# A spectral mixing and SwiGLU kernel: its build-time scheduler, its kinds, and the engine of its setup copies are changed

## The chip, the cores and the metric

The kernel runs on one core of a Trainium2 chip. The metric is the device time of one execution in microseconds. The core's engines run side by side: TensorE (PE) multiplies matrices and accumulates into eight PSUM banks, VectorE (DVE), ScalarE (ACT) and GpSimd (POOL) work on elements, SyncE (SP) and some others issue DMAs. Each engine works through its own list of instructions in the order in which the program was built; an instruction waits on semaphores for others.

## The reference

```python
def _attn_ref(x):                      # x: 8 x 3008 x 256, float32
    X = np.fft.fft(x, axis=1)
    X = np.fft.fft(X, axis=2)
    return X.real

def _moe_ref(x, w_gate, w_val, w_out): # 24064 tokens, 256 -> 1536 -> 256
    g = x @ w_gate
    silu = g * (1.0 / (1.0 + np.exp(-g)))
    val = x @ w_val
    return silu * val @ w_out
```

The real part of a two-dimensional Fourier transform of each of eight sequences is fed, token by token, through a gated feed-forward layer.

## The kernel before, in words

**Symmetry.** A row of the transform at one frequency and the row at the mirrored frequency share an even part and an odd part. The kernel keeps these two parts, transposed, in tiles Pt (even) and Qt (odd) of up to 512 columns. The transform over the 256 features is folded into the weights: Wp is the cosine transform of the weights, Wq the sine transform, Wm is -2 Wq with some rows masked, Wg is Wm of the gate halved. A column's plus side is Wp Pt + Wq Qt, its mirror, the minus side, is the same with the odd part's sign turned. There are 24 tiles of columns.

**Units.** The feed-forward layer is walked tile by tile, and in a tile by twelve blocks f of 128 hidden rows. Such a unit (t, f) has a gate bank and a value bank in PSUM. How a bank's two sides are made is its kind, a digit in the table KINDS (one line for each tile: twelve gates, twelve values, twelve products):

- kind 0: matmuls with Wp and Wq give the plus side, which is read; a third matmul with Wm on top turns the bank into the minus side.
- kind 1: after the Wp matmul DVE copies the even part out and adds a constant row to it (L1123); after the Wq matmul the bank is the plus side, and DVE makes the minus side as 2 x even - bank (gate L1177, value L1191). Two matmuls.
- kind 2: ACT writes the constant row into the bank first (the seed, L1113), the matmul with Wp adds to it, ACT copies the even part out (L1120); then one matmul with Wg or Wm, and DVE's difference. Two matmuls.

ACT takes the silu of both sides (L1138, L1169, L1180). The plus product is D, made by DVE from the bank (L1161), or P, where ACT copies the value out (L1154) and POOL multiplies (L1157). The minus products of two blocks are multiplied together on POOL (L1198), or on DVE where the value has kind 0. The products h are then multiplied with the output weights Wo, 12 matmuls of 256 columns for each 128 tokens (class OWork, L1225); ACT evicts the result (L1231, L1234) and SP stores it.

**The next sequences.** While the units run, POOL folds the rows of the sequences to come (L207 to L231), TensorE transforms them (transform_op, L1356), ACT copies the odd half out of PSUM (L1367) and DVE writes the results into Pt and Qt (the puts, L1381; those of the first sequence are L683).

**The prologue.** Up to the first units all is ordered by hand, in the lines L287 to L738. The trigonometric tables are computed on the chip: angles (L395), magnitude (L399), then cosine and sine on ACT, a negated copy of table columns on ACT (L411), a weighting with a per-row constant (weigh, L408). place() copies rows of the input into PSUM with 0/1 matmuls (L469), sums() adds them on DVE (L478), giving SA for the rows at the front and SC for the rest; heads() makes the first columns from them (L487, L488). fold_d (L535) and direct (SBc, L572) fold over features; half_folded and unfolded are the first sequence's transform matmuls; half_w (L503 to L507) makes the first 512 columns of Wp and Wq, load_w (L421) issues the DMAs of the weights on POOL's queue, columns in three groups. The second and third groups (weight_op, L1410 to L1416) are made while the first units run, as are the second half of the tables (angle_op, weigh_op, odd_op, L1436 to L1487).

**The scheduler.** From the first unit on, every instruction is an entry of class Sched: its engine, an assumed length, what it reads and writes, a category. The entry's due time is the sum of TensorE lengths before it plus a shift of its category (SHIFT). The planner plays the assumed lengths through: for every engine it looks among the entries due within WINDOW of that engine's first one and takes the one that can start earliest. It thereby fixes the order of each engine's list and which PSUM bank or work buffer each entry gets. Delays for semaphores (SEM), for the end of an instruction behind its issue (TAIL) and for a second waited-for engine (EVENT), and when each engine comes free (BEGIN, EARLY), are constants:

```python
o.at = o.clock + SHIFT[o.cat][min(5, int(o.clock / 96))]
t = x.end + SEM[e] if x.eng != e else x.free if e == "PE" else x.end
```

Of the kernel before, what the change touches and what calls it, by code (L numbers as in the profile page):

```python
# [12 lines left out]
F32 = mybir.dt.float32  # L13
# [17 lines left out]
EARLY = {**{("Q", i): 14.0 for i in range(2)}, **{("S", i): 14.0 for i in range(6, 11)}}  # L31
KINDS = [
    "000000000000 000000000000 DDDDDDDDDDDD",
    "000000000000 001111001111 DDDDDDDDDDDD",
    "000000000000 111111111111 DDDDDDDDDDDD",
    "000200022200 121211211211 DPDDDDDDPDDD",
    "000002000220 121122111221 DDDDDDDDDDDD",
    "000000002020 212112112111 DDPDDPDDDDDD",
    "000002020200 121122221111 DDDDDPDDDDPD",
    "220000002200 121212111111 DDDDDDDDPDDD",  # L40
    "200000000000 121112111122 DDDDPDPDDDDD",
    "200220020200 112111121212 DDPDPDDDDPDD",
    "020200000022 111111212211 DPPDPDDDPDDP",
    "000002002000 121111121111 DDPPDDDPDDPD",
    "022200002002 112121112112 DDDDDDPPDPDD",
    "000220200200 121111221211 PDDDDDDPPDDD",
    "000000200002 112211212111 DDPDDPDDDDDD",
    "200222002000 111122211111 DDPDDDDDDPDD",
    "200020000200 111122111211 DDDDDPPDPDDD",
    "220000200002 111121121121 PDDDDDPDDPDD",  # L50
    "022200200020 111112221111 DPPDDDPDDDDP",
    "002002000200 212111111211 DDDPPPDDDDDP",
    "020222000002 111111111111 PDPDPDDDDPPD",
    "222022000020 111111111122 DPDPDDDDDPDD",
    "202000000200 111121111112 PDDPPPDDDDDP",
    "202020202022 112211111212 DDDDPDPDDPDD",
# [8 lines left out]
def kernel(  # L65
# [248 lines left out]
    fall_c(0, 1, q)  # L314

# [181 lines left out]
    def half_w(h, k, pool, nm):  # L497
# [6 lines left out]
        if k:  # L504
            nc.scalar.copy(dst[:, :, fs], ps)
        else:
            nc.vector.tensor_copy(dst[:, :, fs], ps)  # L507
# [56 lines left out]

    def direct(k):
# [19 lines left out]
    load_w(0, (1,))  # L585
    d_tables()
# [3 lines left out]
    if 0:  # L590
        warm(0)
# [7 lines left out]
    X3c = XC.rearrange("p a q d -> p (a q d)")  # L599
# [1010 lines left out]
```

## Time and profile before

| | us |
|---|---|
| median of 3 runs | 611.87 (611.11 to 611.89) |
| the profiled execution | 612.4 |
| its span, first to last instruction | 610.5 |
| PE busy | 602.7 (99%) |
| ACT busy | 567.3 (93%) |
| DVE busy | 558.0 (91%) |
| POOL busy | 541.8 (89%) |
| DMA moved | 57.72 MB, mean 95 GB/s |

The busy times are shares of the span. A matmul's end is modelled in the profile and overlaps the next one's start, so a TensorE that is shown busy is not TensorE at its peak; starts of successive matmuls say more. A group row of the profile reads: line, engine, operation, tiles written and read, shape, count, then busy time and the mean length in ns, then the idle time of the engine just before and what ended it. A row of the timeline reads: start, length (both us), engine, line, operation, and in brackets an idle stretch before it. The chain of waits follows the work that ended last back to the start. A row of windows gives the stretch, its length, and busy time with counts of PE, weight loads, DVE, ACT and POOL, the granted TensorE clock, the share of the DMA engines and GB/s. In this kernel's profile one instruction's length on ACT or DVE includes a part that overlaps the next one's, so here too starts are the better measure of what an engine can take.

### The profile page before, as it was taken

The page shows a single profiled execution, that of the slowest core. Times are in us where ns is not written, and L with a number is a line of the kernel's source. Part 1 is how long each engine was busy: PE and PEld are TensorE (multiplying, and loading weights), DVE is VectorE, ACT ScalarE, POOL GpSimd, SP SyncE. Part 2 cuts the span into 40 slices and gives each one's busy share as a digit, 9 for nine tenths or more (in the row PEclk, how much of TensorE's full clock was granted, in tenths as well). Part 3 has the DMA queues.
Part 4 walks back from the last instruction along what each step waited for, and adds up shares of the span by engine and source line. Part 5 has one row for each costly group of instructions (what it writes and reads, how often), then busy time and mean ns, then how long its engine had stood idle before and what let it go on. Part 6 is the DMA issues. An engine that isn't in the chain of part 4 may idle for free.

```text
span 610.5 us, 12689 instructions
## 1 busy us (share of the span) xinstructions
PE 602.7 (99%) x4071; PEld 395.1 (65%) x4071; DVE 558.0 (91%) x1028; ACT 567.3 (93%) x1104; POOL 541.8 (89%) x498
## 2 busy tenths in 40 slices
PE   8999999999999999999999999999999999999997
PEld 6546666666666666666666666666666666666686
DVE  8999998988999998998999898999999899999882
ACT  7687659999999999999999999999999999999995
POOL 8888999999889999999999999998999868766772
PEclk9999999999999999999999999999999999999999
DMA  9955536344514423445214411235211111211112
GB/s 226 143 101 109 151 104 183 99 125 130 146 53 107 132 60 117 116 129 130 62 46 116 123 49 60 72 84 152 59 48 53 45 53 47 61 44 55 58 54 79
DMA packets 50737, 57.72 MB, mean 95 GB/s; under 512 B 7256, under 2 KB 37724, under 8 KB 50670
## 3 DMA queue, kind: packets, MB, share of 16 engines
q1 hardware_dynamic: 47016, 53.78, 32.2%
q0 software_dynamic: 3216, 2.36, 2.9%
q10 hardware_dynamic: 438, 0.77, 0.5%
q8 instruction: 32, 0.52, 0.4%
q14 instruction: 35, 0.29, 0.2%
HBM read 29.43 MB, written 24.65 MB: 89 GB/s over the span
## 4 chain that ended last, share of the span: by engine, by line
PE 90%; ACT 2%; DVE 2%; POOL 2%; DMA 2%; issue 1%; ACTq 0%; POOLq 0%
PE ps L1057 46%; PE ps L1225 40%; PE ps L1356 4%; DMA XA<-in_moe_w_val_dram 2%; PE ps L641 1%; POOL EOA L535 1%; ACT ps L1113 0%; ACT sv0q L1169 0%; DVE hm L1185 0%; DVE rr L395 0%; DVE hp L1161 0%; POOL XA L421 0%; ACT sv1q L1169 0%; POOL W L421 0%; ACT wk3s L1180 0%
## 5 line engine op out<-in xcount | busy, mean ns | idle before, releaser
L1057 PE MATMUL ps<-Pt,Wp 128*128 128x512 bf16 (+2 forms) x576 | 206.9, 374 | 0.7 <-DVE Qt L683 0.3
L1225 PE MATMUL ps<-Wo,hm 128*128 128x256 bf16 (+2 forms) x1140 | 165.1, 272 | 0.0
L1225 PE MATMUL ps<-Wo,hp 128*128 128x256 bf16 (+2 forms) x1140 | 164.5, 272 | 0.4 <-ACT wk4s L1231 0.2
L1057 PE MATMUL ps<-Qt,Wq 128*128 128x512 bf16 (+2 forms) x427 | 156.4, 375 | 0.0
L1225 PEld LDWEIGHTS <-hm 128*128 128x128 bf16 (+2 forms) x1140 | 111.8, 98 | 59.4 <-issue 3.0
L1225 PEld LDWEIGHTS <-hp 128*128 128x128 bf16 (+2 forms) x1140 | 111.8, 98 | 56.3 <-issue 4.3
L1198 POOL TENSOR_TENSOR hm<-sv0q 128x1024 bf16<-128x1024 f32 (+2 forms) x68 | 126.7, 1863 | 22.0 <-ACT sv0q L1169 11.2
L1198 POOL TENSOR_TENSOR hm<-sv1q 128x1024 bf16<-128x1024 f32 (+2 forms) x68 | 126.7, 1864 | 20.3 <-ACT sv1q L1169 12.7
L1113 ACT ACTIVATE ps<-bc,w 128x512 f32<-128x512 bf16 (+2 forms) x149 | 110.4, 755 | 0.7
L1057 PE MATMUL ps<-Qt,Wm 128*128 128x512 bf16 (+2 forms) x293 | 104.4, 375 | 0.2 <-DVE hp L1161 0.2
L1057 PEld LDWEIGHTS <-Wp 128*128 128x128 bf16 x576 | 56.2, 98 | 32.5 <-issue 1.7
L1169 ACT ACTIVATE sv0q<-ps 128x512 f32<-128x512 f32 (+2 forms) x102 | 70.6, 713 | 1.2 <-PE ps L1057 0.8
L1169 ACT ACTIVATE sv1q<-ps 128x512 f32<-128x512 f32 (+2 forms) x90 | 64.1, 718 | 2.9 <-POOL hm L1198 2.0
L1057 PEld LDWEIGHTS <-Wq 128*128 128x128 bf16 x427 | 41.6, 98 | 26.8 <-issue 3.7
L1057 PEld LDWEIGHTS <-Wm 128*128 128x128 bf16 x293 | 28.5, 98 | 11.7 <-issue 0.2
L207 POOL TENSOR_TENSOR SDf<-XA 128x1020 f32<-128x1020 f32 x14 | 33.0, 2360 | 0.7 <-DMA XC<-in_x_dram 0.7
L1057 PE MATMUL ps<-Qt,Wg 128*128 128x512 bf16 (+2 forms) x80 | 29.7, 371 | 0.0
L217 POOL TENSOR_TENSOR Af<-EOf 128x516 f32<-128x516 f32 (+1 forms) x22 | 24.5, 1112 | 0.3
L214 POOL TENSOR_TENSOR EOf<-SDf 128x512 f32<-128x512 f32 (+1 forms) x22 | 24.1, 1097 | 0.0
L211 POOL TENSOR_TENSOR EOf<-SDf 128x512 f32<-128x512 f32 (+1 forms) x22 | 24.0, 1091 | 0.0
L207 POOL TENSOR_TENSOR SDf<-XC 128x1020 f32<-128x1020 f32 (+1 forms) x8 | 18.8, 2356 | 2.3 <-DMA XA<-in_x_dram 2.3
L1356 PE MATMUL ps<-Tab,St 128*128 128x376 bf16 (+1 forms) x64 | 20.0, 322 | 0.0
(434 smaller groups left out, 1410.5 us busy)
## 6 DMA issues: line engine op xcount, KB each, us to landing
XA<-in_x_dram SPq DMA_DIRECT2D x30, 256.0 KB
XA<-in_x_dram SPq DMA_DIRECT2D x112, 64.0 KB
XC<-in_x_dram SPq DMA_DIRECT2D x30, 120.0 KB
XC<-in_x_dram SPq DMA_DIRECT2D x105, 32.0 KB
bc<-br SPq DMA_DIRECT2D x21, 128.0 KB
out_dram<-wk8s SPq DMA_DIRECT2D x15, 128.0 KB
St<-Fc SPq DMA_DIRECT2D x14, 128.5 KB
out_dram<-wk2s SPq DMA_DIRECT2D x11, 128.0 KB
```

What stands on the lines that cost most here:

```text
L207: tt(F[:, :, 1:D], up[:, :, 1:D], down[:, :, D - 1:0:-1], op=Alu.add)
L211: tt(E[:, :, 0:P], F[:, :, P:0:-1], F[:, :, P:D], op=Alu.add)
L214: tt(O[:, :, 0:P], F[:, :, P:0:-1], F[:, :, P:D], op=Alu.subtract)
L217: tt(Af[r], EOf[r, :, 0:2, :], EOf[r, :, 2:4, :], op=Alu.add)
L535: ptt(EOA[:, eo, a0:a0 + 2, :, 0:P], s_[:, :, :, P:0:-1], s_[:, :, :, P:D], op=(Alu.add, Alu.subtract)[eo])
L641: nc.tensor.matmul(ps[:, e], Z0[:, q, k, :], Tab[:, c, q, 0, e], start=False, stop=True, skip_group_check=True)
L1057: nc.tensor.matmul(ps[:, :n], Wt[:, gv, fs], src[:, :n], start=start, stop=stop, skip_group_check=True)
L1113: nc.scalar.activation(bank(k)[:, :self.wp], bc[self.t][:, :self.wp], AF.Copy, scale=w0[:, gv, self.f:self.f + 1])
L1169: return lambda: nc.scalar.activation(self.silu(self.sm, w), src()[:, :w], AF.Silu)
L1198: lambda: nc.gpsimd.tensor_tensor(tiles_of(t)[1][:, f - 1:f + 1, :w], pair(self.vm)[:, :, :w, 1], pair(self.vm)[:, :, :w, 0], op=Alu.mult),
L1225: nc.tensor.matmul(bank(ko)[:n, j * D:(j + 1) * D], hts[t][minus][:, f, c:c + n], Wo[:, f, :], start=(f == 0), stop=(f == nF - 1))
L1356: nc.tensor.matmul(ps[:, cols], l, r_, start=(i == 0), stop=(i == len(mms) - 1), skip_group_check=True)
```

## The change

1. **Kinds.** The table is another one: gates of kind 0, 1, 2 were 208, 0, 80 and become 195, 37, 56; values 16, 203, 69 become 18, 190, 80; products made by ACT and POOL 61 become 72.
2. **The planner.** Shifts come in 24 bins of 24 us in place of 6 of 96 (the old ones were the same in all bins). An engine other than PE that uses its own earlier result is charged its end and a semaphore, and this counts as a wait. Lengths are changed, some ends get their own delay (lat), WINDOW, TAIL, EVENT, BEGIN, EARLY and the ring's start are other constants. Where the value is of kind 0 and the gate is not, the plus product is entered in the unit's second half.
3. **Setup work from DVE to ACT**: the casts of Wp (half_w and weight_op), magnitude in angle_op (as an absolute value), weigh_op, odd_table. Halving Wm of the values moves from unit 37 to 25, making Wg from 24 to 13.
4. **The prologue's order.** half_folded(0, 2) goes ahead of place(); start_acc(1), the first fold_d(1) and half_folded(1, 0) go earlier; the clearing of unused rows is split in two, one DMA right behind the loads and one behind a memset that comes earlier; load_w(0, (1,)), which loads the value columns of the first weight group, and d_tables come later; first_columns computes what the heads need with two small additions, so that they need not wait for all of SC; half_w(0, 0) goes ahead of unfolded(1), half_w(0, 1) behind row0; the last sum of SC goes behind transform(0, 0, (1,)).

The core of the diff:

```diff
@@ quarter_rows
-        tt(B_[:, 1], O[:, 0:2, 0:P], O[:, 2:4, 0:P], op=Alu.subtract)
+        tt(B_[:, 1, :, 1:P], O[:, 0:2, 1:P], O[:, 2:4, 1:P], op=Alu.subtract)
@@ half_w
-        if k:
-            nc.scalar.copy(dst[:, :, fs], ps)
-        else:
-            nc.vector.tensor_copy(dst[:, :, fs], ps)
+        nc.scalar.copy(dst[:, :, fs], ps)
@@ prologue
+    clear_rest(0, xf[:, 7 * D:8 * D])
...
+    hc = tp.tile([P, 2, 2, 1], F32, name="hc")
+    def first_columns():
+        for a in range(2):
+            vtt(hc[:, a], psC[a][:, :, 0:1], XC0[:, 2 + a, ::-1, 0:1], op=Alu.add)
...
-    load_w(0, (1,))
-    d_tables()
     sums(SA, 1, XA, psA)
     start_acc(0)
     half_folded(0, 0)
+    half_folded(0, 2)
     psC = place(XC0, putC, 2, ((psG, "g"), (psV, "v")))
-    half_folded(0, 2)
-    for a in (0, 2):
-        fold_d(1, a)
+    start_acc(1)
+    fold_d(1, 0)
+    half_folded(1, 0)
+    zeros = Af.rearrange("p a b d -> p (a b d)")[:, 0:D]
+    nc.gpsimd.memset(zeros, 0.0)
+    clear_rest(1, zeros)
+    load_w(0, (1,))
+    d_tables()
+    fold_d(1, 2)
     direct(0)
     direct(1)
-    start_acc(1)
+    first_columns()
...
-    for a in (0, 2):
-        half_folded(1, a)
+    half_folded(1, 2)
     load_w(1)
...
-    heads(nc.gpsimd, SC[:, 0, 0, :, 0:1], SC[:, 0, 1, :, 0:1], CEc)
+    heads(nc.gpsimd, hc[:, 0], hc[:, 1], CEc)
...
-    for k in range(2):
-        half_w(0, k, psO, "o")
+    half_w(0, 0, psO, "o")
     unfolded(1, SBc)
     for q in range(2):
         row0(0, q, acc[1][q])
-    sums(SC, 1, XC0, psC)
+    sums(SC, 1, XC0, psC, (0,))
     transform(0, 0, (1,), acc)
+    half_w(0, 1, psO, "o")
+    sums(SC, 1, XC0, psC, (1,))
@@ planner
-    WINDOW = {"DMA": 14.0, "PE": 9.378, "ACT": 14.0, "DVE": 12.28, "POOL": 11.566, "SP": 5.558}
+    WINDOW = {"DMA": 5.66, "PE": 7.62, "ACT": 14.0, "DVE": 14.0, "POOL": 14.0, "SP": 7.13}
-    TAIL = {"PE": 0.163, "ACT": 0.118, "DVE": 0.08, "POOL": 0.02, "SP": 0.0, "DMA": 0.0}
+    TAIL = {"PE": 0.163, "ACT": 0.099, "DVE": 0.083, "POOL": 0.044, "SP": 0.0, "DMA": 0.0}
-    EVENT = 0.06
-    BEGIN = {"DVE": 1.2, "ACT": 0.7, "POOL": 14.0, "PE": 0.0, "SP": -4.0}
+    EVENT = {"ACT": 0.055, "DVE": 0.072, "POOL": 0.06, "PE": 0.03}
+    BEGIN = {"DVE": 0.6, "ACT": 1.3, "POOL": 13.1, "PE": 0.0, "SP": -6.6}
-                o.at = o.clock + SHIFT[o.cat][min(5, int(o.clock / 96))]
+                o.at = o.clock + SHIFT[o.cat][min(23, int(o.clock / 24))]
-                    t = x.end + SEM[e] if x.eng != e else x.free if e == "PE" else x.end
+                    t = x.free if x.eng == e and e == "PE" else x.end + SEM[e]
-                        if g != e and g != "x":
+                        if (g != e or e != "PE") and g != "x":
-        return n / 1200 + (0.094 if sbuf else 0.063) + 0.12 * ptr
+        return n / 1200 + (0.088 if sbuf else 0.0605) + 0.1245 * ptr
-                S.add("ACT", act_us(self.wp, 1) - 0.01, fn, r=[self.bc, (("w0",), 0)], w=[k], new=[k[0]], cat=cat,
+                S.add("ACT", act_us(self.wp, 1), fn, r=[self.bc, (("w0",), 0)], w=[k], new=[k[0]], cat=cat, lat=0.08,
-                S.add("ACT", act_us(self.wp) - 0.025, by_act, r=[k], w=[e], new=[e[0]], cat="esc" if gv else "egc")
+                S.add("ACT", act_us(self.wp), by_act, r=[k], w=[e], new=[e[0]], cat="esc" if gv else "egc")
-    FOLD_US = (2.0, 1.06, 1.06, 1.15, 1.24, 1.55)
+    FOLD_US = (2.475, 1.047, 1.047, 1.057, 1.204, 1.345)
@@ setup during the units
-                nc.vector.tensor_copy(dst[:, gv, fs], bank(ko))
+                nc.scalar.copy(dst[:, gv, fs], bank(ko))
-        S.add("DVE", 0.6, lambda: magnitude(raO[:, ch], rrO[:, ch]), ...
+        S.add("ACT", 0.72, lambda: nc.scalar.activation(raO[:, ch], rrO[:, ch], AF.Abs), ...
-        S.add("DVE", 0.45, lambda: weigh(NOO, NTAB), w=[(("Tab",), ("o", 1))])
+        S.add("ACT", 0.52, lambda: nc.scalar.activation(Tab[:, 1, 1, :, NOO:NTAB], Tab[:, 1, 1, :, NOO:NTAB], AF.Copy, scale=wC), ...
-        nc.vector.tensor_copy(Tab[r, c, :, :, NCE:NCE + GH], src[:, :, ::-1] if half else src)
+        nc.scalar.copy(Tab[r, c, :, :, NCE:NCE + GH], src[:, :, ::-1] if half else src)
-        if i == FIRST + 1:
+        if i == 2 * nF + 1:
             S.add("ACT", 1.36, lambda: nc.scalar.activation(Wm[:, 1], Wm[:, 1], AF.Copy, scale=-0.5), ...
-        if i == 2 * nF:
+        if i == nF + 1:
             S.add("DVE", 0.5, lambda: vts(Wg[:, 0], Wm[:, 0], scalar1=-0.5, scalar2=None, op0=Alu.mult), ...
```

More of the change, by code (lines that the diff above doesn't have):

```diff
@@ L57 @@
+    "000212122211 111122111111 PPPDPPDPPDDD",
 ]
@@ L902, in run @@
             lanes = [-9.0] * 8
[L903 removed]
+            ring = -2.0
             def slot_time(s, e):
@@ L966, in ready @@
                         own = max(now, key=lambda g: RANK.get(g, 0))
-                        at = max([at] + [waits[g][1] + EVENT for g in now if g != own])
+                        at = max([at] + [waits[g][1] + EVENT[e] for g in now if g != own])
                 if commit:
@@ L1431, in weight_op @@
             else:
-                S.add("DVE", 0.6, even, r=[ko], w=[(("Wp",), (fc, gv))])
+                S.add("ACT", act_us(T), even, r=[ko], w=[(("Wp",), (fc, gv))])
     raO = SDf.rearrange("p a d -> p (a d)")[:, 0:4 * G].rearrange("p (c q n) -> p c q n", c=2, q=2)
@@ L1474, in d0_op @@
         r = [(("st", b), k) for k in range(2)] if part else [(("cp", b), (q, 0)) for q in range(2)]
-        S.add("POOL", 0.2, fn, r=r, w=[(("Z0",), part)])
+        S.add("POOL", 0.147, fn, r=r, w=[(("Z0",), part)])
     def halve_tables():
```

136 lines of the change are left out of this document (65 added, 71 removed), and 28 rows, old and new, of the table SHIFT.

## The prediction

> **What bounds the kernel now.** I read the busy totals first, then the windows by stage, then the chain of waits, then the timeline around the stalls it shows.
>
> ```profile
> PE 602.7 (99%) x4071; PEld 395.1 (65%) x4071; DVE 558.0 (91%) x1028; ACT 567.3 (93%) x1104; POOL 541.8 (89%) x498
> 0.00:25.00 25.00, 22.47 (x157) 15.49 (x158) 21.99 (x74) 15.78 (x27) 19.82 (x42) 1.00 0.87 182
> 25.00:50.00 25.00, 23.94 (x142) 11.74 (x140) 24.14 (x43) 21.68 (x41) 22.13 (x35) 1.00 0.65 116
> 50.00:92.00 42.00, 41.76 (x280) 27.41 (x278) 40.61 (x64) 26.99 (x50) 38.85 (x41) 1.00 0.49 128
> 92.00:250.00 158.00, 157.67 (x1060) 103.03 (x1058) 145.59 (x267) 151.71 (x293) 153.08 (x137) 1.00 0.42 116
> 250.00:600.00 350.00, 349.85 (x2380) 231.40 (x2378) 324.41 (x582) 348.13 (x690) 306.66 (x247) 1.00 0.26 73
> PE 90%; ACT 2%; DVE 2%; POOL 2%; DMA 2%; issue 1%; ACTq 0%; POOLq 0%
> ```
>
> In a window row the columns behind the length are PE, weight loads, DVE, ACT and POOL with their counts, then the clock granted to TensorE (1.00 throughout). TensorE fills 99% of the span and 90% of the chain: it is the bound. But from 250 to 600 us ScalarE is busy 348.13 of 350 (0.505 us for each of its 690 instructions), so the kernel stands on two limits at once there, with DVE at 93%. Before 92 us it is the other way round: DVE is nearly full (24.14 of 25, 40.61 of 42) and ScalarE has 9.2 + 3.3 + 15.0 = 27.5 us idle.
>
> TensorE's busy time overstates its work, since the modelled ends overlap. Its work is better read from starts:
>
> ```profile
> 44.96 3.36 PE ps L1057 x16
> 137.27 1.31 PE ps L1225 x12
> 300.41 0.38 PE L1057 MATMUL ps<-Qt,Wq 128*128 128x512 bf16 x1
> 300.63 0.38 PE L1057 MATMUL ps<-Pt,Wp 128*128 128x512 bf16 x1
> 53.79 0.59 PE L1057 MATMUL ps<-Qt,Wm 128*128 128x512 bf16 x2
> 54.62 0.27 PE L1225 MATMUL ps<-Wo,hp 128*128 128x256 bf16 x1 [0.24 <-ACT wk4s L1231]
> 581.53 0.30 PE L1057 MATMUL ps<-Qt,Wg 128*128 128x328 bf16 x1
> 581.73 0.30 PE L1057 MATMUL ps<-Qt,Wq 128*128 128x328 bf16 x1
> ```
>
> A 512-column matmul costs 0.216 us (300.41 to 300.63), an output one 1.31 / 12 = 0.109, a 328-column one 0.138 by its width. A distance longer than the pitch is a stall: two matmuls from 53.79 should have ended at 54.22, the next began at 54.62, so 0.40 was lost; the last stall of this kind, at 581.53, lost 0.20 - 0.14 = 0.06. Between these two lie all but one of the 53 stalls over 60 ns that stand behind 50 us; together they are 6.35 us. Ahead of 50 us it is 4.4 us. These two sums, and the matmul columns themselves, are all that the change can work on, unless it brings new stalls.
>
> **The change, part by part.**
>
> *Kinds.* Counting the tables: gates of kind 0/1/2 go from 208/0/80 to 195/37/56, values from 16/203/69 to 18/190/80, P products from 61 to 72. Kind 0 takes three matmuls, 1 and 2 take two: -13 for the gates, +2 for the values, so 11 fewer, which by tile widths is ten of 512 columns, two of 320, and one more of 480. At 0.216 each this is **-2.2 us** on the engine that bounds. No cover is needed for it, unless TensorE then waits.
>
> The other engines, in tiles 3 to 23:
>
> ```profile
> L1113 ACT ACTIVATE ps<-bc,w 128x512 f32<-128x512 bf16 x130 | 98.0, 768 | 0.7
> 303.89 0.74 DVE L1123 SCALAR_TENSOR_TENSOR wk9s<-bc,w,ps 128x512 f32<-128x512 bf16 x1
> 304.55 0.68 DVE L1177 SCALAR_TENSOR_TENSOR wk10s<-wk4s,ps 128x512 f32<-128x512 f32 x1
> 305.46 1.27 POOL L1157 TENSOR_TENSOR hp<-wk0s,wk3s 128x512 bf16<-128x512 f32 x1
> ```
>
> Kind 2 falls there from 149 to 127 (each a seed and an even copy on ScalarE) and 11 value copies come: -44 + 11 = -33 ScalarE instructions, at 0.505 us -16.7 us. DVE gains 31 even copies of kind 1 (304.55 - 303.89 = 0.66 us each), 9 gate differences and loses 11 products (about 0.6 each by starts): +19.3 us. POOL gains 11 products of 1.27: +14 us. So ScalarE's near-full state ends, and DVE, 324.41 of 350 in the late window, comes to about 338 there with its share of the 19.3 (350 of the 515 us behind 92, so 13), and to 344 with all of it. POOL goes from 306.66 to about 317. None passes TensorE's 350, so I charge them nothing by themselves; what cover they lose is in the stalls below.
>
> *The planner.* Lengths of copies and seeds drop their discounts (a 512-column copy 0.465 to 0.487, a seed 0.600 to 0.612), same-engine results cost a semaphore step, priorities get 24 bins, windows change. Nothing in this adds a matmul; it changes who waits in the 6.35 us of stalls. ScalarE's relief removes the cause of those stalls that end on a seed, an eviction or a plus-side silu; those that end on DVE (products, differences) do not go, and get worse by DVE's +19.3. Bounds: all of it goes (-6.3), or it doubles (+6). I take a third gone, **-2.0**: nearer to the first, as the fullest engine is relieved by more than half of what TensorE has to spare, and the others are not filled.
>
> *Prologue.* Rows around the first units:
>
> ```profile
> 13.80 0.67 PE L469 MATMUL ps<-XC,putC 128*128 128x512 f32 x1 [1.16 <-DVE SA L478]
> 12.50 0.73 POOL L421 DMA_DIRECT2D W<-in_moe_w_val_dram  x1
> W<-in_moe_w_val_dram POOLq DMA_DIRECT2D x1, 256.0 KB, 4.6
> XA<-in_moe_w_val_dram POOLq DMA_DIRECT2D x2, 256.0 KB, 9.6
> 20.17 0.68 DVE L507 CAST Wp<-ps 128x512 bf16<-128x512 f32 x1
> 20.77 1.28 DVE L478 TENSOR_TENSOR SC<-ps,XC 128x512 f32<-128x512 f32 x2
> 22.09 1.27 DVE L683 TENSOR_TENSOR Qt<-ps,od 128x188 bf16<-128x188 f32 x6
> 23.41 0.77 PE L1057 MATMUL ps<-Pt,Wp 128*128 128x480 bf16 x3 [0.35 <-DVE Qt L683]
> 20.34 0.20 POOL L487 TENSOR_TENSOR CEc<-SC 128x2 bf16<-128x2 f32 x1 [2.21 <-DVE SC L478]
> 22.54 9.81 DMA XA<-in_moe_w_val_dram
> 32.40 0.62 PE ps L1410 x2
> ```
>
> Steady units begin at 23.41, behind the Qt puts that begin at 22.09 on DVE. After the change the Wp cast (20.77 - 20.17 = 0.60) is on ScalarE, and one of the four SC sums (1.28 / 2, about 0.6) stands behind the puts: DVE's list ahead of them is 1.2 us shorter, two tiny first-column additions put back about 0.2, and TensorE's own order (unfolded(1) now behind half_w(0,0), half_w(0,1) behind row0) takes some more. By the list the puts start near 21.4. The matmuls put in front of place C (half_folded(0,2), 13.80) fill the 1.16 us that TensorE waits there. I take **-0.5**. Against it: POOL issues W's value columns about 1.4 us later (12.50 to some 13.9), behind two fold_d, a memset and the first clear; SP's stores of zeros for XC go ahead of that and share the queues. With the 4.6 us of its own row it lands near 18.5 and half_w(0,0) needs it at 19; with the 9.6 us of the later value columns it lands at 23.5, and TensorE's order is stuck at half_w with unfolded(1) behind it: +3.9. Other end -1.3, the whole of DVE's 1.2 and the rest of the wait. I stand near the own row.
>
> *Second and third weight columns.* POOL waits 2.21 us at 20.34 for the SC sums before it issues them; the heads now read the first-column sums, so both issues come about 1.9 us earlier. In the chain the value columns' 9.81 us from 22.54 end in the weight matmuls at 32.40. TensorE's stalls ahead of these two groups (at 29.0 and 31.7, 0.57 and 0.53) can both go: **-1.0**; bounds 0, if the transfers wait in the same crowd (DMA share 0.87 and 0.65 in the first windows), and -1.1.
>
> *Masks, weights and tables to ScalarE.* The nearest rows:
>
> ```profile
> L1413 DVE CAST Wp<-ps x4: 678/685/692, 25.4 to 33.0; 128x512 bf16<-128x512 f32 x4
> L1416 ACT CAST Wq<-ps x4: 586/596/606, 25.9 to 33.5; 128x512 bf16<-128x512 f32 x4
> L411 ACT ACTIVATE Tab<-Tab x2: 823/829/835, 9.5 to 13.1; 128x752 bf16<-128x752 bf16 x2
> L1484 DVE COPY Tab<-Tab x4: 356/943/1511, 44.5 to 51.8; 64x752 bf16<-64x752 bf16 x4
> L408 DVE TENSOR_SCALAR Tab<-Tab,wC x1: 1292/1292/1292, 37.6 to 37.6; 128x752 bf16<-128x752 bf16 x1
> L399 DVE TENSOR_SCALAR SDf<-XA x2: 535/582/629, 26.0 to 31.6; 128x752 int32<-128x752 int32 x2
> ```
>
> Two Wp casts, four more (L1413), two magnitudes, one weigh, four table copies leave DVE: 6 x 0.685 + 2 x 0.58 + 1.29 + 4 x 0.94 = 10.3 us. On ScalarE they cost 6 x 0.596 + 7 x 0.83 = 9.4 us. Tile 2's new kinds add nine seeds and nine copies there, 18 x 0.505 = 9.1. Together 18.5 of the 27.5 us that ScalarE idles before 92 us, so it fits, though less so where it is needed: the silus of the first tiles stand behind these casts. TensorE hardly stalls there on DVE even now, so the relief is worth little. **0**, bounds +3 (three table operations of 0.83 and a cast caught in front of silus) and -0.8 (the stalls at 38.9 and 54.0).
>
> The Trainium skill, "ScalarE: Activation LUTs", Rules for kernel authors, tells the author to put such work on VectorE, per element up to about 3x faster in bf16. The rows above do not bear that out for these shapes (0.596 on ScalarE against 0.685 on DVE for the cast); by the rule the step would not be free, and that result is the last rival.
>
> *Wm's halving* moves from unit 37 to 25, Wg from 24 to 13: one instruction each, beside other work, nothing. *Tail:* the last output products are the same, 0.
>
> **Sum.** -2.2 - 2.0 - 0.5 - 1.0 = -5.7 us. The profiled execution took 612.4 us (span 610.5, 1.9 around it), 0.5 above the median of 611.87. So 606.7 as profiled, 606.2 as a median.
>
> **Rivals.**
> (A) The planner buys nothing: the stalls after 50 us stay as they are, only matmul columns and the prologue count: -3.7, 608.2. For it: each stall is small (0.06 to 0.4 us) and scattered, so no one engine owns them. Against it: ScalarE at 348.13 of 350.
> (B) DVE takes ScalarE's place. A kind 1 gate holds its PSUM bank through an even copy, a matmul, a difference and a silu of both sides, two of these on DVE; with DVE near 98% late, banks come free late and the next unit's first matmul waits. From four microseconds of stall growth on it eats the gains (-3.7 without the stall term); with stalls doubled, +6, 614, and up to 616 with POOL's +14 beside it. Against it: by sums no engine is full.
> (C) W's value columns land late and the prologue loses instead of gaining: landing 8.5 us after the issue, +2.8 in place of -0.5, the rest as forecast, 609.5. For it: the value columns behind took 9.6. Against it: the same chunk took 4.6.
> (D) Moved work costs three times DVE's time on ScalarE: 10.3 x 3 = 31 us, with tile 2's 9.1 it is 40 in 27.5 idle: 12.5 over, 606.7 + 12.5 = 619.
>
> **How the numbers follow.** 0.2% (1.2 us) is about what a measurement of this kernel tells from no change: 610.65 to 613.1. Chances: forecast 0.55, A 0.20, C 0.09, B 0.14, D 0.02. Faster: the forecast, nearly all of A (0.18) and half of C make 0.78. Same: 0.07 from the rest of A and C and the weak end of B. Slower: 0.15. The low end takes two thirds of the stalls (-4.2), the prologue -1.3, the weight waits -1.1, the early relief -0.8 and the columns -2.2: -9.6, 602.3. The high end goes past A and most of C, to 610.7; B and D above it hold 0.16.
>
> **What would show it.** Right: 11 fewer L1057 matmuls, ScalarE's late window under 340 of 350, steady units at about 22.8, no stall at the weight matmuls near 30 us, stalls after 50 us near 4 us. Wrong: DVE over 97% late and TensorE waiting on L1123, L1177 or L1161 (B); TensorE waiting on W ahead of 20 us (C); ScalarE full before 92 us with silus late (D); the stall sum above 6 us.

## The result

The changed kernel takes 607.81 us (median of 6 runs, 607.02 to 609.88) against 611.73 (6 runs, 610.78 to 612.93): ratio 0.9941, 95% interval 0.9921 to 0.9961, 0.6% faster and clear of the 0.2% that can be told. Forecast were 606.2 in a range of 602.3 to 610.7. The profiled execution took 607.03 us, span 605.1, against 612.4 and 610.5. All that follows compares these two. They are 5.4 us apart, the medians 3.9: the profiled execution of before is slower than its median, the changed kernel's faster, so the rows below show somewhat more of a gain than there is.

The busy totals, the five windows and the chain of the changed kernel, columns as before:

```profile
PE 594.9 (98%) x4060; PEld 393.2 (65%) x4060; DVE 563.6 (93%) x1043; ACT 566.6 (94%) x1102; POOL 550.0 (91%) x508
0.00:25.00 25.00, 20.96 (x154) 13.87 (x155) 20.57 (x73) 15.95 (x27) 21.93 (x45) 1.00 0.98 197
25.00:50.00 25.00, 22.23 (x130) 10.60 (x129) 18.11 (x30) 23.60 (x46) 19.68 (x32) 1.00 0.59 111
50.00:92.00 42.00, 42.00 (x275) 26.92 (x273) 38.12 (x63) 38.45 (x72) 36.38 (x39) 1.00 0.41 113
92.00:250.00 158.00, 158.00 (x1077) 104.86 (x1076) 151.12 (x277) 149.33 (x292) 154.35 (x139) 1.00 0.44 117
250.00:600.00 350.00, 350.00 (x2420) 235.72 (x2418) 335.72 (x604) 338.36 (x668) 317.70 (x258) 1.00 0.27 75
PE 93%; DMA 4%; POOL 1%; ACT 1%; SPq 1%; issue 0%; DVE 0%; DVEq 0%
```

The gain is behind 92 us: 1077 matmuls where there were 1060, 2420 where there were 2380, in the same stretches, with TensorE shown busy throughout. Ahead of 50 us the changed kernel is worse: 154 + 130 matmuls against 157 + 142, and DMA has become 4% of the chain. In distances between starts, beyond the pitch and counted from 60 ns up as in the prediction (profiled executions):

| | before | changed | difference |
|---|---|---|---|
| matmul columns | | | -2.2 |
| stalls ahead of 50 us | 4.0 | 8.3 | +4.2 |
| stalls behind 50 us | 6.4 | 0.8 | -5.5 |
| distances under 60 ns, all | 6.9 | 5.4 | -1.6 |
| last matmul ends | 607.0 | 601.7 | -5.3 |

(The small distances are what is left of TensorE's whole distance to its pitches, 17.4 and 14.5 us, without the stalls. The rows add up to -5.1; 0.2 is not placed.)

Most of the -1.6 is not the change's. Out of TensorE's first 52 matmuls, a stretch of the timeline before and then changed:

```profile
4.20 1.38 PE L341 MATMUL ps<-sel 128*128 128x128 bf16 x11
4.30 1.17 PE L348 MATMUL ps<-sel 128*128 128x128 bf16 x18
```

These matmuls of 128 columns start 0.107 us apart at first and 0.056 us apart later. The step comes at 7.0 us before and at 4.2 us in the changed kernel; in the seven other profiled kernels with this order of the prologue and this issue of W it comes between 4.5 and 6.8 us, so it differs from one execution to the next. From TensorE's first matmul (1.02 us in both) to the first unit the changed kernel takes 1.1 us more, although its stalls there are 2.5 us more: some 1.4 us of the small distances lie ahead of the first unit, and only some 0.4 us behind it (the 0.2 that is not placed among them).

Where the time ahead of 50 us goes is read from the changed kernel's timeline (rows of several engines, in order of time), its DMA issues (the last figure is us to landing) and its chain:

```profile
9.43 0.76 SPq L318 DMA_DIRECT2D XC<-XC  x1
13.26 0.82 PE L527 MATMUL ps<-Tab,EOb 128*128 128x377 bf16 x4 [1.07 <-ACT EOb L540]
13.79 0.73 POOL L428 DMA_DIRECT2D W<-in_moe_w_val_dram  x1
14.60 3.77 SPq L190 DMA_DIRECT2D XC<-in_x_dram  x7
18.24 0.22 POOL L494 TENSOR_TENSOR CEc<-hc 128x2 bf16<-128x2 f32 x1
19.73 0.38 PE L510 MATMUL ps<-W,CD 128*128 128x256 bf16 x2 [1.14 <-DMA W<-in_moe_w_val_dram]
22.35 1.27 DVE L690 TENSOR_TENSOR Qt<-ps,od 128x188 bf16<-128x188 f32 x6 [1.33 <-ACT od L685]
23.79 1.18 PE L1085 MATMUL ps<-Pt,Wp 128*128 128x480 bf16 x5
27.07 0.83 ACT L1470 ACTIVATE SDf<-XA 128x752 f32<-128x752 f32 x1 [0.35 <-DVE XA L402]
28.41 0.36 PE L1085 MATMUL ps<-Pt,Wp 128*128 128x480 bf16 x1 [0.49 <-ACT wk2s L1198]
34.96 0.61 PE L1441 MATMUL ps<-XA,CD 128*128 128x512 bf16 x2 [1.64 <-DMA XA<-in_moe_w_val_dram]
```

```profile
XA<-in_moe_w_val_dram POOLq DMA_DIRECT2D x2, 256.0 KB, 12.9
W<-in_moe_w_gate_dram POOLq DMA_DIRECT2D x1, 256.0 KB, 6.3
W<-in_moe_w_val_dram POOLq DMA_DIRECT2D x1, 256.0 KB, 5.9
```

```profile
20.44 14.47 DMA XA<-in_moe_w_val_dram
```

Of before, the clears and the row loads in the timeline, and W's gate columns:

```profile
15.82 1.51 SPq L605 DMA_DIRECT2D XC<-Af  x2
17.38 4.51 SPq L190 DMA_DIRECT2D XC<-in_x_dram  x2
W<-in_moe_w_gate_dram POOLq DMA_DIRECT2D x1, 256.0 KB, 4.6
```

The matmuls put ahead of place C now wait themselves, 1.07 us at 13.26 for a copy on ScalarE, where TensorE waited 1.16 us before. W's value columns land 5.9 us behind their issue, not 4.6, and hold TensorE 1.14 us (1.7 to 2.4 us in those seven other kernels); DVE has its shorter list done and now waits 1.33 us for ScalarE's copy of TensorE's later result. Steady units begin at 23.79 (before: 23.41, with a first matmul at 22.70). The heads no longer wait and the third weight group is issued at 20.44, 2.1 us earlier; but it takes 14.47 us in place of 9.81 and lands 2.6 us later than before. By the trace's landings twelve of this DMA's sixteen parts are there by 25.2 us, and TensorE waits for the last four, which come from 32.5 to 34.9. SP issues the first of the two clears at 9.43 (15.82 before) and the first load of the next sequences' rows at 14.60 (17.38). At 27.07 a magnitude on ScalarE stands in front of a silu for which TensorE waits 0.49 us.

### The profile page after: what moved, and what is told of

It is laid out like the page before. It is cut to its first block, busy times and chain, and to the rows that moved or that the text cites. A ratio compares the mean times of both kernels' runs of the same rounds, so it can differ in the third digit from the quotient of the medians.

```text
span 605.1 us, 12684 instructions
## 1 busy us (share of the span) xinstructions
PE 594.9 (98%) x4060; PEld 393.2 (65%) x4060; DVE 563.6 (93%) x1043; ACT 566.6 (94%) x1102; POOL 550.0 (91%) x508
## 4 chain that ended last, share of the span: by engine, by line
PE 93%; DMA 4%; POOL 1%; ACT 1%; SPq 1%; issue 0%; DVE 0%; DVEq 0%
PE ps L1085 46%; PE ps L1256 41%; PE ps L1387 4%; DMA XA<-in_moe_w_val_dram 2%; DMA XA<-in_x_dram 1%; PE ps L648 1%; POOL EOA L539 1%; SPq L190 0%; DVE SA L485 0%; POOL XA L398 0%; PE ps L1441 0%; ACT SDf L1470 0%; ACT Tab L412 0%; POOL W L428 0%; POOL XA L428 0%
## 5 line engine op out<-in xcount | busy, mean ns | idle before, releaser
L1085 PE MATMUL ps<-Pt,Wp 128*128 128x512 bf16 (+2 forms) x576 | 203.9, 375 | 0.7 <-ACT wk2s L1198 0.5
L1256 PE MATMUL ps<-Wo,hp 128*128 128x256 bf16 (+2 forms) x1140 | 162.1, 273 | 0.0
L1085 PE MATMUL ps<-Qt,Wq 128*128 128x512 bf16 (+2 forms) x440 | 160.8, 375 | 0.0
L1229 POOL TENSOR_TENSOR hm<-sv1q 128x1024 bf16<-128x1024 f32 (+2 forms) x67 | 124.8, 1863 | 14.8 <-ACT sv1q L1198 8.5
L1085 PE MATMUL ps<-Qt,Wm 128*128 128x512 bf16 (+2 forms) x293 | 106.0, 376 | 0.4 <-DVE hp L1190 0.2
L1141 ACT ACTIVATE ps<-bc,w 128x512 f32<-128x512 bf16 (+2 forms) x136 | 96.2, 717 | 0.7 <-DVE hp L1190 0.3
L1085 PEld LDWEIGHTS <-Wp 128*128 128x128 bf16 x576 | 56.3, 98 | 29.7 <-issue 0.8
L1198 ACT ACTIVATE sv0q<-ps 128x512 f32<-128x512 f32 (+1 forms) x90 | 59.5, 670 | 1.3 <-PE ps L1085 1.1
L1085 PEld LDWEIGHTS <-Wq 128*128 128x128 bf16 x440 | 43.0, 98 | 27.0 <-issue 2.5
L1198 ACT ACTIVATE sv1q<-ps 128x512 f32<-128x512 f32 (+2 forms) x87 | 57.7, 676 | 0.0
L1085 PEld LDWEIGHTS <-Wm 128*128 128x128 bf16 x293 | 28.6, 98 | 16.7 <-issue 1.1
L1151 DVE SCALAR_TENSOR_TENSOR wk10s<-bc,w,ps 128x512 f32<-128x512 bf16 (+1 forms) x29 | 21.5, 740 | 0.4 <-PE ps L1085 0.3
L1085 PE MATMUL ps<-Qt,Wg 128*128 128x512 bf16 (+2 forms) x56 | 20.8, 372 | 0.0
L1190 DVE TENSOR_TENSOR hp<-wk3s,ps 128x512 bf16<-128x512 f32 (+1 forms) x27 | 18.4, 680 | 1.8 <-ACT wk3s L1166 1.2
```

Of the source, the lines that this page charges most:

```text
L1085: nc.tensor.matmul(ps[:, :n], Wt[:, gv, fs], src[:, :n], start=start, stop=stop, skip_group_check=True)
L1141: nc.scalar.activation(bank(k)[:, :self.wp], bc[self.t][:, :self.wp], AF.Copy, scale=w0[:, gv, self.f:self.f + 1])
L1151: nc.vector.scalar_tensor_tensor(work(e)[:, :self.wp], bc[self.t][:, :self.wp], w0[:, gv, self.f:self.f + 1], bank(k)[:, :self.wp], op0=Al ...
L1190: lambda: nc.vector.tensor_tensor(tiles_of(t)[0][:, f, :wp], work(self.sp)[:, :wp], bank(v)[:, :wp], op=Alu.mult),
L1198: return lambda: nc.scalar.activation(self.silu(self.sm, w), src()[:, :w], AF.Silu)
L1229: lambda: nc.gpsimd.tensor_tensor(tiles_of(t)[1][:, f - 1:f + 1, :w], pair(self.vm)[:, :, :w, 1], pair(self.vm)[:, :, :w, 0], op=Alu.mult),
```

## The experiments

All medians; ratios to the kernel before, with 95% intervals; the last columns are TensorE's stalls over 60 ns in each profiled execution. In four of them (kinds only and the three flat ones) some 60 of 4060 matmul records are missing, while the weight loads are complete; there a gap that holds the load of a missing matmul is shortened by its 0.215 us, and counts of matmuls are read from the loads. In k_prologue_old and k_fit_setup_dve 1.7 us of the stalls ahead of 50 us are no waits but a stretch at half clock (last section).

| kernel | us | ratio | ahead of 50 us | behind |
|---|---|---|---|---|
| before | 611.73 | | 4.0 | 6.4 |
| changed | 607.81 | 0.9941 (0.9921 to 0.9961) | 8.3 | 0.8 |
| k_kinds_only | 626.71 | 1.0241 (1.0221 to 1.0261) | 4.9 | 21.3 |
| k_lengths_old_flat | 625.59 | 1.0224 (1.0205 to 1.0244) | 9.3 | 16.0 |
| k_shift_flat | 617.06 | 1.0085 (1.0068 to 1.0103) | 8.7 | 9.0 |
| k_kinds_old_flat | 615.38 | 1.0057 (1.004 to 1.0073) | 8.9 | 5.6 |
| k_fit_kinds_old | 611.85 | 0.9995 (0.9984 to 1.0006) | 9.6 | 1.9 |
| k_fit_kinds_new | 607.62 | 0.9932 (0.9915 to 0.9948) | 6.7 | 1.6 |
| k_setup_dve | 614.76 | 1.0044 (1.0028 to 1.006) | 7.5 | 8.0 |
| k_fit_setup_dve | 608.34 | 0.9947 (0.993 to 0.9964) | 8.2 | 3.6 |
| k_prologue_old | 607.71 | 0.9916 (0.9886 to 0.9945) | 7.8 | 1.7 |
| k_clears_late | 606.45 | 0.9901 (0.9872 to 0.9931) | 8.5 | 1.2 |
| k_wval_early | 605.96 | 0.9901 (0.9869 to 0.9932) | 6.6 | 1.3 |
| k_fit_wval | 606.24 | 0.9906 (0.9891 to 0.9921) | 6.2 | 0.9 |

**Did ScalarE's relief take the stalls away?** My theory was that the stalls behind 50 us went because the new kinds leave ScalarE room; the rival, that each engine's order is fitted by lengths and shifts, whatever the kinds. Four kernels without the new shifts tell them apart. The kinds alone, on the kernel before:

```diff
 KINDS = [                          # the changed kernel's table
...
             if V == "0":
                 S.add("PE", ... Wq ...)
-                self.product_p()
+                if G == "0":
+                    self.product_p()
...
             if V == "0":
+                if G != "0":
+                    self.product_p()
```

(In it Wm is halved where it was, behind tile 2, so tile 2's values of kind 2 are made with a weight twice too large; no instruction is left out.)

> The kernel before with the new table of kinds alone (and the plus product of a unit whose gate is not of kind 0 entered in its second half, which such units need). Relief theory (the stalls of TensorE behind 50 us, 6.35 us before and 0.8 after counted over distances more than 60 ns beyond the pitch, went because ScalarE has fewer instructions): stalls fall to 2 us or less, with the 2.2 us of matmul columns 604 to 606. Plan theory (they went because each engine's order is fitted by the lengths and the shifts, whatever the kinds): stalls stay at 6 us or grow, 609 to 612.

The changed kernel with the old shifts:

```diff
-        "eg": (13.68, -16.61, 12.03, ...          # and 20 more categories, 24 bins
+        "eg": (-7.62, -7.62, -7.62, -7.62, -7.62, -7.62),
...
-                o.at = o.clock + SHIFT[o.cat][min(23, int(o.clock / 24))]
+                o.at = o.clock + SHIFT[o.cat][min(5, int(o.clock / 96))]
```

> The changed kernel with the old shifts, the same in all bins; lengths, waits, kinds, prologue and setup stay new. Relief theory: stalls behind 50 us stay near 1 to 2 us, 608 to 609. If the shifts by time bin are what took the stalls away: 5 us or more of stalls, 612 to 614.

The same with the old lengths, windows, ends and waits as well (all of the planner's constants that the diff shows, and its two rules):

```diff
-                    t = x.free if x.eng == e and e == "PE" else x.end + SEM[e]
+                    t = x.end + SEM[e] if x.eng != e else x.free if e == "PE" else x.end
...
-        return n / 1200 + (0.088 if sbuf else 0.0605) + 0.1245 * ptr
+        return n / 1200 + (0.094 if sbuf else 0.063) + 0.12 * ptr
```

> The changed kernel with the old shifts and also the old lengths, windows and rules for an engine's own results; kinds, prologue and setup stay new. Relief theory: as with flat shifts alone, 608 to 610. Plan theory, if lengths and waits matter by themselves: 1 to 3 us slower than flat shifts alone.

And the changed kernel with the old shifts and the old table of kinds:

```diff
-    "000000000000 000000111111 DDDDDDDDDDDD",    # and 22 more rows
+    "000000000000 001111001111 DDDDDDDDDDDD",
```

> The changed kernel with the old shifts and the old table of kinds; lengths, waits, prologue and setup stay new. Relief theory: ScalarE is full again, stalls behind 50 us near the 6.35 of before, and 2.2 us of columns come back: 612 to 615, some 5 us above flat shifts alone. Plan theory: only the 2.2 us of columns more than flat shifts alone.

Windows of the kinds alone, then of the flat shifts with new kinds, then with old kinds:

```profile
92.00:250.00 158.00, 155.86 (x1035) 102.00 (x1049) 146.85 (x269) 148.52 (x284) 151.50 (x135) 1.00 0.42 111
250.00:600.00 350.00, 342.43 (x2239) 220.69 (x2273) 326.74 (x576) 330.30 (x639) 309.12 (x249) 1.00 0.27 73
```

```profile
92.00:250.00 158.00, 156.75 (x1055) 104.39 (x1071) 150.05 (x276) 149.77 (x292) 151.83 (x134) 1.00 0.40 113
250.00:600.00 350.00, 345.08 (x2312) 228.30 (x2346) 334.09 (x598) 335.18 (x658) 315.61 (x257) 1.00 0.27 75
```

```profile
250.00:600.00 350.00, 345.67 (x2333) 230.71 (x2370) 324.74 (x582) 346.07 (x685) 304.79 (x245) 1.00 0.26 73
```

The relief theory falls. The kinds alone make the kernel 15 us slower, with 21.3 us of stalls for 6.4: ScalarE has 20 us free between 250 and 600 us, no engine is full, and yet TensorE gets through 105 weight loads fewer there than before (2273 for 2378). With flat shifts and new lengths the new kinds are 1.7 us slower than the old ones, 617.06 to 615.38, although they have 2.2 us fewer columns: their stalls are 9.0 us, those of the old kinds 5.6, with ScalarE at 335 and 346 us. With the new kinds, the new lengths, windows and rules together are worth 8.5 us under flat shifts (625.59 to 617.06), the shifts 9.3 more (617.06 to 607.81). With no engine full, what is left is what the planner fixes: the order, an instruction that comes too late or too early in its engine's list, and with it the banks and buffers; these two are not told apart. All four kernels came out outside the times that either theory had given: the plan theory had the direction of the first three, not the sizes, and expected the old kinds to be 2.2 us slower than the new ones under flat shifts.

**Is it these shifts, these kinds, or the fit?** The old shifts were the kernel before's own, so flat shifts may simply suit the old kinds. So each list got shifts and windows fitted to it: from the old flat ones, by a random search that keeps what ends earlier in the planner's own play. One edit, another table:

```diff
-    SHIFT = {...}    # the changed kernel's
-    WINDOW = {...}
+    SHIFT = {...}    # fitted to this kernel's list, 24 bins
+    WINDOW = {...}
```

> The changed kernel with the old table of kinds and with shifts and windows fitted anew to that list (a random search that keeps what ends earlier in the planner's own play, from the old flat shifts). If the gain lies in an order fitted to the lengths, and the kinds add only their matmul columns: TensorE's stalls behind 50 us fall from 9.5 us (flat shifts, old kinds) to under 3, and the time lies 2 to 4 us above the changed kernel, 610 to 611.5. If the new kinds are what makes few stalls possible: stalls stay over 5 us, 613 or more.

(The 9.5 us in it does not allow for the missing records and is a slip besides; with flat shifts and old kinds the stalls behind 50 us are the 5.6 of the table.)

> The changed kernel with its own kinds and shifts and windows fitted anew by the same search, from the old flat shifts: another order for the same list. If it is the fit and not those particular shifts: stalls behind 50 us under 2 us and 607 to 609, as the changed kernel. If the shifts in the change hold something that the planner's play does not know: 610 or more.

The late window of the fitted old kinds, then of the new kinds fitted anew:

```profile
250.00:600.00 350.00, 349.93 (x2400) 233.73 (x2399) 327.34 (x586) 348.47 (x692) 305.71 (x246) 1.00 0.27 73
```

```profile
250.00:600.00 350.00, 349.85 (x2414) 234.85 (x2413) 335.22 (x604) 338.28 (x666) 316.90 (x257) 1.00 0.27 74
```

With the old kinds ScalarE is as full as before, 348.47 of 350, and TensorE stalls only 1.9 us behind 50 us, where it stalled 6.4: so a full ScalarE does not by itself make stalls. With another set of fitted shifts the new kinds give 607.62, the changed kernel's time, with 1.6. So the steady stage's gain is the fit, and what the kinds add is seen between the two fitted kernels: 611.85 to 607.62, 4.2 us, of which 2.2 are columns. Most of the rest lies ahead of 50 us (stalls of 9.6 and 6.7 in the profiled executions, which are 5.0 us apart); 1.8 of these 2.9 us are waits for weight DMAs (2.15 and 1.46 us, for 1.81 and none, on W and on the third group's gate columns). How much of it is the first tiles' kinds and how much luck of a plan or of the landings, no run here tells. Kept with this prologue, an order fitted to the old kinds gives nothing at all (0.9995): what it wins behind 50 us goes into the 9.6 us ahead of it.

**Setup copies back on DVE.** Without and with shifts fitted to that list:

```diff
-        nc.scalar.copy(dst[:, :, fs], ps)            # half_w, and weight_op, magnitude, weigh, odd_table alike
+        if k:
+            nc.scalar.copy(dst[:, :, fs], ps)
+        else:
+            nc.vector.tensor_copy(dst[:, :, fs], ps)
```

> The changed kernel with the setup copies (half_w, the second weight groups, magnitude, weigh, odd_table) back on DVE; kinds, lengths, shifts and prologue's order new. By my step (costs nothing on ScalarE, relieves DVE little): within 1 us of the changed kernel. If the early DVE limit was real: DVE full again ahead of 92 us and 2 to 4 us slower. If casts on ScalarE stand ahead of silus and cost: 1 us faster. A changed list also changes the plan behind it, so the windows behind 92 us have to be read beside the total.

> The changed kernel with the setup copies back on DVE, and shifts and windows fitted anew to that list. If moving them to ScalarE was worth nothing and the 614.76 of the unfitted version was only a plan that no longer matched its list: 607 to 609. If DVE really lacks the room ahead of 92 us: 610 or more, with TensorE's stalls ahead of 92 us more than 2 us above the changed kernel's 8.5.

The window from 50 to 92 us of the first, then of the second:

```profile
50.00:92.00 42.00, 40.03 (x252) 24.82 (x253) 37.41 (x63) 32.98 (x62) 33.90 (x37) 1.00 0.34 95
```

```profile
50.00:92.00 42.00, 41.57 (x276) 27.09 (x274) 41.23 (x64) 34.55 (x64) 35.45 (x37) 1.00 0.54 126
```

614.76 looked as if DVE's relief were worth 7 us. But DVE was not even full in that window (37.41 of 42; it was nearly so ahead of it, 23.61 of 25): thirteen instructions on another engine had made the plan fit its list no longer. Fitted, DVE is full (41.23), TensorE has its 276 matmuls, and the time is 608.34, whose interval overlaps that of the fitted kernel with ScalarE's copies (0.9947 to 0.9932). By these medians (607.62 to 608.34) the move by itself is worth 0.7 us, within the noise. That ScalarE's magnitudes can stand in front of a silu is in the rows above; the price was 0.49 us.

**The prologue.** Its order of before, then the two suspects one by one:

```diff
+    load_w(0, (1,))
+    d_tables()
     sums(SA, 1, XA, psA)
     start_acc(0)
     half_folded(0, 0)
-    half_folded(0, 2)
     psC = place(XC0, putC, 2, ((psG, "g"), (psV, "v")))
+    half_folded(0, 2)
...
-    half_w(0, 0, psO, "o")
+    for k in range(2):
+        half_w(0, k, psO, "o")
```

(And so on: the whole prologue hunk of the diff undone.)

> The changed kernel with the prologue's order of before (Wp's casts stay on ScalarE, everything from the first unit on is unchanged). If the new order is what lost time ahead of 50 us (TensorE stalls there 4.0 us before, 8.3 after): steady units at about 23.4 or earlier, weight matmuls not waiting past 33 us, 2 to 4 us faster than the changed kernel, 604 to 606. If the new order saved time and the casts on ScalarE lost it: 0 to 1 us slower than the changed kernel.

```diff
     opposite(1)
+    load_w(0, (1,))
+    d_tables()
     sums(SA, 1, XA, psA)
...
     clear_rest(1, zeros)
-    load_w(0, (1,))
-    d_tables()
```

> The changed kernel with W's value columns (and the small tables behind them) issued where they were issued before, ahead of the second set of SA sums. If the later issue holds TensorE: its 1.1 us wait on W at 19.7 goes, steady units begin at 22.7 instead of 23.8, about 1 us faster, 606.8. If the transfer is slow because others crowd it: no gain, or the wait only moves to the second weight group.

```diff
-    clear_rest(0, xf[:, 7 * D:8 * D])
...
-    clear_rest(1, zeros)
...
     ptt(hd, SA[:, 0, 0:2, :, 0:1], SA[:, 0, 2:4, :, 0:1], op=Alu.add)
+    for hi in range(2):
+        clear_rest(hi, zeros)
```

> The changed kernel with both clearing DMAs issued behind the memset and first heads as before, so that the loads of the next sequences' rows start some 2 us later, at about 17.4 us. If these loads crowd out the weights: the third weight group's value columns land by 32 instead of 34.9 us, and TensorE's 1.8 us stall there shrinks under 0.6, 1.5 to 2.5 us faster. If not: no change of the landing, and the same time within 0.5 us.

Clears late, its timeline (the clears and the row loads on SP, the first units), its DMA issues and a line of its waits (us in total, times, longest):

```profile
13.89 1.50 SPq L318 DMA_DIRECT2D XC<-Af  x2
15.43 4.79 SPq L190 DMA_DIRECT2D XC<-in_x_dram  x5
22.75 1.18 PE L1085 MATMUL ps<-Pt,Wp 128*128 128x480 bf16 x5
```

```profile
XA<-in_moe_w_val_dram POOLq DMA_DIRECT2D x2, 256.0 KB, 11.6
W<-in_moe_w_gate_dram POOLq DMA_DIRECT2D x1, 256.0 KB, 4.4
W<-in_moe_w_val_dram POOLq DMA_DIRECT2D x1, 256.0 KB, 4.8
```

```profile
PE ps L1256 <- DMA Wo<-in_moe_w_out_dram: 1.3, 1, 1.3
```

W's value columns issued early, timeline and DMA issues:

```profile
15.34 5.48 SPq L190 DMA_DIRECT2D XC<-in_x_dram  x7
19.44 0.38 PE L510 MATMUL ps<-W,CD 128*128 128x256 bf16 x2 [0.54 <-DMA W<-in_moe_w_val_dram]
```

```profile
XA<-in_moe_w_val_dram POOLq DMA_DIRECT2D x2, 256.0 KB, 10.0
W<-in_moe_w_gate_dram POOLq DMA_DIRECT2D x1, 256.0 KB, 7.2
W<-in_moe_w_val_dram POOLq DMA_DIRECT2D x1, 256.0 KB, 6.9
```

With both clears behind W's issue, which stands where the changed kernel has it, W lands in 4.8 us and the units begin at 22.75, where I had forecast them. With the issue 1.3 us earlier the transfer itself takes 6.9 and the wait is halved, not gone (first unit at 23.5, expected at 22.7). So W is crowded by another transfer, and the later issue is the smaller part of the wait for it.

My expectation named the row loads for the crowd. The run moved them by 0.8 us, not 2.8 (15.43 for 14.60), and the rows speak for the first clear. W's gate columns are issued at 10.6 us in every kernel, ahead of any row load. They take 4.6 us before and 4.4 with clears late, where the clears come behind; they take 6.3 in the changed kernel and 7.2 with W early, where the first clear is issued ahead of them, at 9.43 and 9.85. With W early the row loads begin at 15.34, as with clears late, so they do not make this difference. In the ten profiled executions with the clear ahead the gate columns take 6.3 to 7.8 us, in the four others 4.1 to 4.6. The packets of the traces agree: 64 packets of 1,024 bytes on SP's queue, the 64 KB of one clear, move between 12.5 and 15.8 us in those ten, beside W's; the first packet of the row loads moves at 18.4 us in the changed kernel.

The third group is another matter. Its value columns land at 34.9 us in the changed kernel, at 33.0 with clears late (I had expected 32) and at 31.2 with W early; there the earlier issue does more, row loads do move beside it, and what crowds it is not shown.

And what goes earlier somewhere goes later elsewhere: with clears late the output weights come late and TensorE waits 1.3 us for them. Both variants are faster than the changed kernel by their medians, by 1.4 and 1.9 us, though their intervals overlap with its own. With the whole old order the first unit starts at 22.55; the median, 607.71, is no better than the changed kernel's, the ratio, 0.9916, is, and the intervals overlap. In its profiled execution, the slowest of five, TensorE waits 2.1 us for Wo and then loses 1.7 us at half clock. My expectation that the new order lost 2 to 4 us is not borne out in its size. That the plan behind it is made for the new order's arrivals may be a reason; no run here shows it.

The last kernel puts W early, sets the assumed arrivals near those of that version, and fits again:

```diff
-    for fc, gv, at in ((1, 0, 1.4), (1, 1, 4.4), (2, 0, 6.0), (2, 1, 8.5)):
+    for fc, gv, at in ((1, 0, 0.8), (1, 1, 3.7), (2, 0, 6.6), (2, 1, 9.0)):
...
-    S.add("DMA", 0.01, lambda: None, w=[(("Wo",), 0)], lat=18.0)
+    S.add("DMA", 0.01, lambda: None, w=[(("Wo",), 0)], lat=20.5)
```

> The changed kernel with W's value columns issued early, the weights' assumed arrivals set to those seen in that version, and shifts and windows fitted anew. If the stall at the third weight group and ahead of the first units are cured by an earlier issue and a plan that knows the arrivals: TensorE's stalls ahead of 50 us fall from 8.3 to about 6, and 604.5 to 606, under the 605.96 of the version without the fit. If arrivals vary too much for a fixed plan: 606 to 608.

606.24: as the one without a fit, not under it as I had expected. TensorE's stalls ahead of 50 us fall to 6.2 us, behind it to 0.9, and the interval of the ratio is the narrowest among the kernels that are clearly faster than before, 0.9891 to 0.9921. It is the version I would keep.

## Why the prediction was right, and where it was not

The time lay in the range, and the kernel was faster, by 3.9 us in the medians where 5.7 were forecast (607.81 for 606.2). That it came so near is luck: two errors of opposite sign. The terms as measured, -2.2 for columns, -5.5 and -0.4 for the planner, +0.6 for the prologue and +2.2 up to 50 us, add up to the -5.3 by which the last matmul ends earlier in the profiled executions.

- *Kinds, columns, -2.2:* right, 11 fewer L1085 matmuls and 2.2 us by pitch. Load on the others: ScalarE 338.36 of 350 (under 340 as said), DVE 335.72 (338 said), POOL 317.70 (317).
- *Planner, -2.0 of 6.35:* the step that failed in size and in cause. It gave -5.5, and some -0.4 in small distances behind the first unit; the bound of -6.3 was the nearer one. I argued from ScalarE's relief. k_fit_kinds_old has ScalarE as full as before and 1.9 us of stalls, so that argument was wrong: the stalls were a matter of order, which a plan with new lengths and fitted bins repairs. The view that showed it was already there: stalls of 0.06 to 0.4 us on three engines, which I used to speak for rival A.
- *Prologue, -0.5:* +0.6 (23.79 where the steady units began, with 23.41 less one pitch before). DVE's list did get shorter, DVE then waited 1.33 us on ScalarE. The matmuls moved ahead of place C did not fill TensorE's 1.16 us there: they wait 1.07 us themselves. Rival C's place and mechanism were right, W landed late, but in 5.9 us, not 8.5, and what crowded it were the stores of zeros that the prediction had named there, the first of them above all; I had stood by the 4.6 us and given C 0.09.
- *Second and third weights, -1.0 (0 to -1.1):* wrong in sign: +0.7 at the weight matmuls themselves (1.8 us of stalls for 1.1), and +2.2 in all between first unit and 50 us (4.3 us of stalls for 2.0), the rest in short waits for ScalarE and DVE. The issues came 2.1 us earlier as said, the last landing 2.6 us later. My bounds left a loss out; the row that spoke for one, 9.6 us against 4.6 for the same size, stood in the prediction.
- *Setup on ScalarE, 0:* within the noise by k_fit_setup_dve, 0.7 us. The prices held (L1470 and L1516 0.83, casts 0.59 to 0.62 in the median, weigh 0.92 for 0.83). The Trainium skill's rule in "ScalarE: Activation LUTs", Rules for kernel authors, is written for relu, max, min, add and mul; of the moved work weigh is such a multiplication. The prediction took the rule for all of the moved work. Weigh takes 0.92 us on ScalarE, and on DVE 1.29 before, 0.48 in k_setup_dve and 1.58 in k_fit_setup_dve: DVE can be nearly twice as fast here, and slower as well. The casts, which the rule does not name, are shorter on ScalarE (0.59 for 0.685). None of the moved work cost three times its time on DVE, ScalarE was busy 78.0 of the 92 us, and rival D fell with that.
- *Rival B* did not come: DVE is at 96% in the late window and TensorE at 350.00. A's time, 608.2, is nearest to the measured one, by accident; its mechanism, stalls that stay, is the opposite of what happened.
- *Two slips of the working* that change no term: the stalls ahead of 50 us are 4.0 us where the prediction has 4.4, and rival D's 619 starts from the profiled 606.7, not from the median 606.2.

## What to carry to other kernels

When the bounding engine waits in many short stalls on several engines, count neither their busy shares nor the relief of the fullest one: the order can be at fault, as here, and a build-time plan with new lengths and shifts fitted to its list can remove nearly all of it (6.4 to 0.8 us here). Such a plan is fitted to one list; a change of a dozen instructions or of a table under the old plan measures the misfit (k_setup_dve 614.76, k_kinds_only 626.71), so a part is only priced after the plan is fitted to it. And an earlier DMA issue is worth what its landing shows: in a crowded prologue, ask which transfers start earlier beside it or just ahead of it.

## What the runs showed of the hardware

In some executions TensorE ran at half clock after a wait. The old prologue's profiled execution, timeline, then windows of 1 us (the figure before the last two is the granted clock; the row from 46 to 47 is left out):

```profile
43.92 0.60 PE L1252 MATMUL ps<-Wo,hp 128*128 128x256 bf16 x4 [2.09 <-DMA Wo<-in_moe_w_out_dram]
46.15 0.61 PE L1081 MATMUL ps<-Qt,Wm 128*128 128x480 bf16 x1
46.55 0.61 PE L1081 MATMUL ps<-Pt,Wp 128*128 128x480 bf16 x1
```

```profile
43.00:44.00 1.00, 0.08 (x1) 0.11 (x2) 0.00 (x0) 1.00 (x2) 1.00 (x1) 1.00 0.44 96
44.00:45.00 1.00, 1.00 (x7) 0.61 (x7) 0.17 (x1) 0.17 (x1) 1.00 (x1) 0.81 0.54 123
45.00:46.00 1.00, 1.00 (x6) 0.65 (x5) 1.00 (x3) 0.00 (x0) 1.00 (x3) 0.50 0.53 127
47.00:48.00 1.00, 1.00 (x5) 0.51 (x4) 0.00 (x0) 0.36 (x1) 0.92 (x2) 0.50 0.52 115
48.00:49.00 1.00, 1.00 (x7) 0.53 (x6) 0.41 (x1) 0.68 (x2) 0.92 (x2) 0.99 0.51 119
```

After a wait of 2.1 us the clock falls to 0.50 for about 3.4 us, 480 columns take 0.40 us from start to start instead of 0.20, and some 1.7 us are lost. In k_fit_setup_dve a wait of 2.1 us on W did the same (half clock from 21.5 to 25.0 us); waits of 2.2 us in k_fit_kinds_old and 2.4 us in k_shift_flat, on W too, did not. The Trainium skill, "TensorE: Matmul & The Clock Gate", Part 1, has the clock fall after an idle window of about 3.4 us that runs free; here 2.1 us were enough in two executions, while the length of the slow stretch agrees. It explains part of the spread between runs of one kernel: the old prologue's five runs took 605.95 to 609.87 us, and the profiled one is the slowest. A wait of 2 us in a prologue can cost nearly twice.
